# Lower halves of the hidden activations moved from GpSimd to VectorE, and eight accumulator banks dealt out anew

## The chip, the cores and the metric

The kernel runs on one core of a Trainium2 chip. The metric is device time in microseconds (us) of one execution; lower is better. The engines are named as the profile names them: PE is TensorE (matmul), PEld its weight load, DVE is VectorE, ACT is ScalarE, POOL is GpSimd, SP is SyncE, which issues most of the DMAs. Matmul results stand in eight banks of PSUM; POOL does not read them in this kernel.

## The reference

Three layers in a row, on batches of 576 tokens with 512 features, 8 batches in all:

```
q_s = softmax(q, over features); k_s = softmax(k, over tokens)
x   = q_s @ (k_s^T @ v)                      # linear attention, 8 heads of 64
x   = x + relu(layer_norm(x) * g @ w_ch1) @ w_ch2      # 512 -> 2048 -> 512
out = sum over the top 2 of 4 experts of gate * causal_attention(x; wq, wk, wv) @ wo
```

All of it is float32. The kernel splits each float32 operand of a matmul into a high and a low half (type fp32r), and adds three products (high x high, high x low, low x high). The low half is the operand minus its high half, so every operand that a matmul reads costs one pass for the high half and one for the low half.

## The kernel before, in words

The work has three stages. Up to about 250 us the first two batches go through the attention layer and the feed-forward layer, and the weights are prepared. From about 250 to 808 us the batches 2 to 7 go through the feed-forward layer ("fast" batches), one batch in about 90 us, while beside it the attention layer and the layer norm of the next batch are made. From 808 us on the expert layer runs. The change touches the second stage alone.

A fast batch has three groups. In a group (`fast_group`) four blocks of 128 hidden columns are made by seven products of half-size matrices instead of eight; the products run j = 0 to 6, each for i = 0 and 1, and each of these is 6 matmuls into one bank. The products accumulate into three banks by turns: `pa` takes j = 0, 2, 4 and 6, `pc` takes j = 1 and 3, `pb` takes j = 5. Between products, ACT copies a running sum out (`copy`, L1330, tiles `tmp`), and DVE adds such a copy to a later running sum (`total`, L1343). Four of the finished hidden blocks belong to the second half of the tokens (h = 1, tile `hid`), four to the first half (h = 0, they lie in tile `xw_a`). `out_` (L1333) makes relu and the two halves of each. For h = 0 that is `relu_split` (L311): ACT writes relu as the high half (L312), DVE subtracts it and writes the low half (L313). For h = 1 it was three instructions: ACT makes relu in place (L1338), ACT copies it as the high half (L1339), POOL subtracts and writes the low half (L1340).

After the group comes `second` (L1395): eight sums, four for h = 1 and then four for h = 0, each of 12 matmuls into one bank, which DVE then adds to `xT` (L1406). The first of them reads `hid`. In order of need these are `hid` block 0, 2, 1, 3.

The eight banks: four of pool `ps_acc` (acc0 to acc3), two of `ps_m`, two of `ps_y`. Before the change, `pa` had acc0 and acc1 (by i), `pc` and `pb` acc2 and acc3; the eight sums went through one bank of `ps_m` and acc2, acc3, acc0, acc1, in the order that `SBANK` gives. The other bank of `ps_m` was kept for the layer norm's variance `pvar` (`lnbank`). The attention work beside the groups took its banks through `psy` (L340) from the two banks of `ps_y`.

That attention work is done in units, one for two heads of a batch (`Heads`, L419): the pieces name their matmuls `pkm` (L463, L481), `pq` (L548), `pkv` (L554 and L191) and `po` (L191), and the steps of VectorE between them are L453, L499, L505 (row maximum, row sum, reciprocal of q), L449, L472, L490 (k), L540, L571, L572, L581 (halves of the results). POOL makes L456 and L510 of a unit, ACT L475, L494, L537, L577, L598.

SP loads k and q of a later unit (L399, L401) when the buffer of an earlier unit is read, v (L412, L414) when the `pkv` of the unit before it is done, and the prepared weights of the products (`w_r`, L1308) into a ring of five tiles, each when the product that used the tile before is done. SP issues in the order of the program text.

The instructions of PE, DVE, ACT and POOL are put in order by a scheduler that goes through the whole program, by data, buffers and its own estimates of durations; each engine then runs its list in order and waits at an instruction whose inputs or buffers aren't there. A wait so holds up all that stands behind it on that engine.

Of the kernel before, what the change touches and what calls it, by code (L numbers as in the profile page):

```python
# [7 lines left out]
F32 = mybir.dt.float32  # L8
# [3 lines left out]
AF = mybir.ActivationFunctionType  # L12
ALU = mybir.AluOpType
# [5 lines left out]
P = 128  # L19
# [31 lines left out]
FAST = 2  # L51
# [88 lines left out]
def tile_kernel(ctx: ExitStack, tc: tile.TileContext, q, k, v, g_ln, w1, w2, w_gate, wq, wk, wv, wo, out):  # L140
    nc = tc.nc
# [11 lines left out]
    T = S // NH  # L153
# [12 lines left out]
    def raw(ap):  # L166
        return ap.bitcast(F32)
# [42 lines left out]
    ps_m = ctx.enter_context(pool("ps_m", 2, space=PSUM))  # L210
# [100 lines left out]
    def relu_split(ps, h, lo):  # L311
        nc.scalar.activation(h, ps, AF.Relu)  # L312
        nc.vector.scalar_tensor_tensor(lo, ps, 0.0, raw(h), op0=ALU.max, op1=ALU.subtract)  # L313
# [21 lines left out]
    lp = p1r.enter_context(pool("ln", side="right"))  # L335
    ap = p1r.enter_context(pool("a", 2, side="right"))

    spare, idle, lnbank = [], [], []

    def psy(name):  # L340
        if spare:

            spare.append(spare.pop(0))
            if spare[-1] is not None:
                return ps_acc.tile([P, 512], F32, tag=spare[-1], name=name)
        return ps_y.tile([P, 512], F32, tag="y", name=name)


# [284 lines left out]
    class Norm:  # L633
# [25 lines left out]
            nc.vector.tensor_tensor(self.s[:, 1], self.t, raw(self.s[:, 0]), op=ALU.subtract)  # L659

        def mean(self, nm):
            ps = (lnbank[0] if lnbank and nm == "pvar" else psy(nm))[:, :T]
            setattr(self, nm, ps)
            mean_of(ps, self.s)

# [530 lines left out]
    NG = FSPLIT // 4  # L1196
# [76 lines left out]
    def last_space():  # L1273
        x_pair(XORD[5:])
        p1b.close()
        mixp = p1.enter_context(pool("mix"))
        later.append(mixp)
        xslot["b12"] = mixp.tile(XSL, F32R, tag="b12", name="xw_b")
        t = mixp.tile([P, 4, 2, T], F32R, tag="hid", name="hid")
        hid1.extend(t[:, i] for i in range(4))  # L1280
        ring[MIDB] = mixp.tile(WSL, F32R, tag="w", name="w_r")
        qt_odd.append(mixp)
        stream.use(0, before_last + 7, ring)
        stream.fill(-1)
        for _ in range(3):
            t = raw(hp.tile([P, 2, T], F32R, tag="hh", name="tmp", bufs=3))
            temps.extend([t[:, 0], t[:, 1]])
        lnbank.append(ps_m.tile([P, 512], F32, tag="m", name="pvar"))

    class Stream:  # L1290

# [19 lines left out]

    stream = Stream()
    def bank(name, n):
        if n < 0:
            if not main:
                main.append(ps_m.tile([P, 512], F32, tag="m", name="acc"))
            return main[0][:, :T]
        return ps_acc.tile([P, 512], F32, tag=f"acc{n}", name=name)[:, :T]

    main = []  # L1320
    SBANK = (-1, 2, 3, 0, 1, -1, 2, 3)

    def fast_group(b, gr):

        base = (b - FAST) * 7 * NG + 7 * gr
        box = [{} for _ in range(2)]

        def copy(ps, i, k):
            t = temps[3 * i + k]
            nc.scalar.activation(t, ps, AF.Copy)  # L1330
            return t

        def out_(src, i, n, h):  # L1333
            u = (hid0, hid1)[h][2 * i + n]
            if h == 0:
                relu_split(src, u[:, 0], u[:, 1])
                return
            nc.scalar.activation(src, src, AF.Relu)  # L1338
            nc.scalar.activation(u[:, 0], src, AF.Copy)  # L1339
            nc.gpsimd.tensor_tensor(u[:, 1], src, raw(u[:, 0]), op=ALU.subtract)  # L1340

        def total(ps, t):
            nc.vector.tensor_tensor(t, ps, t, op=ALU.add)  # L1343
            return t

        def product(j, i):
            d = box[i]
            nm = ("a", "c", "a", "c", "a", "b", "a")[j]
            begins = nm not in d
            if begins:  # L1350
                d[nm] = bank("p" + nm, i if nm == "a" else 2 + i)
            x, w = xslot[XORD[j]], stream.got[base + j][:, i]
            for c in range(2):
                onto(d[nm], w[:, 0, c], x[:, 0, c], begins and c == 0, False)
                onto(d[nm], w[:, 0, c], x[:, 1, c], False, False)
                onto(d[nm], w[:, 1, c], x[:, 0, c], False, c == 1)
            if j == 0:
                d["t1"] = copy(d["a"], i, 0)
            elif j == 1:
                d["v5"] = copy(d["c"], i, 1)  # L1360
            elif j == 2:
                d["u2"] = copy(d["a"], i, 2)
            elif j == 3:
                out_(total(d["c"], d["u2"]), i, 0, 1)
            elif j == 4:
                out_(total(d["a"], d["v5"]), i, 1, 1)
            elif j == 5:
                out_(total(d["b"], d["t1"]), i, 0, 0)
            else:
                out_(d["a"], i, 1, 0)  # L1370
            if i == 1:
                stream.fill(base + j)

        return [(6, lambda j=j, i=i: product(j, i)) for j in range(7) for i in range(2)]

    def plain_group(b):

        parts = (("b11", "b21"), ("b12", "b22"))

        def one(f, h):  # L1380
            while wide.at < 2 * (f - FSPLIT) + 2:
                wide.step()
            ps = bank("psh", (0, 1, 2, 3, -1)[(4 * (1 - h) + f) % 5])
            for c in range(NDC):
                wh, wl = (w1s[f][:, i, c, :] for i in (0, 1))
                x = xslot[parts[h][c // 2]]
                mm(ps, wh, x[:, 0, c % 2], c == 0, False)
                mm(ps, wh, x[:, 1, c % 2], False, False)
                mm(ps, wl, x[:, 0, c % 2], False, c == NDC - 1)
            u = (hid0, hid1)[h][f - FSPLIT]  # L1390
            relu_split(ps, u[:, 0], u[:, 1])

        return [(12, lambda f=f, h=h: one(f, h)) for h in (1, 0) for f in range(FSPLIT, NFC)]

    def second(b, f0, final):  # L1395

        def one(h, c):
            ps = bank("acc", SBANK[4 * (1 - h) + c])
            sl = slice(c * P, (c + 1) * P)
            for n, i in enumerate((0, 2, 1, 3)):  # L1400
                wt, u = w2s[f0 + i], (hid0, hid1)[h][i]
                mm(ps, wt[:, 0, sl], u[:, 0], n == 0, False)
                mm(ps, wt[:, 0, sl], u[:, 1], False, False)
                mm(ps, wt[:, 1, sl], u[:, 0], False, n == 3)
            xs = xTs[b][:, :, h * T:(h + 1) * T]
            nc.vector.tensor_tensor(xs[:, c], xs[:, c], ps, op=ALU.add)  # L1406
            if final and b == LAST:
                if h not in x2s_last:
                    x2s_last[h] = x_hl(xhlp, "x2")
                x2 = x2s_last[h]  # L1410
                split(xs[:, c], x2[:, 0, c], x2[:, 1, c])
            elif final and c == NDC - 1:
                nc.scalar.dma_start(out=xp_d[b, h], in_=xs)

        return [(12, lambda h=h, c=c: one(h, c)) for h in (1, 0) for c in range(NDC)]
# [79 lines left out]
    n = 2 * HALF + HALF  # L1495
# [3 lines left out]
    m = mixes[FAST]  # L1499
# [5 lines left out]
    for b in range(FAST, B):  # L1505
        if b < LAST:
            slots, n = fronts.pop(b + 1), END
            if b + 2 < B:
                fronts[b + 2] = front(b + 2)
                begin(b + 2, slots, n)  # L1510
        else:
            slots, n = {}, 4 * NFC
            p1r.close()
            x2s_last[0] = t = x_hl(xtp, "x2")
            t = t.rearrange("p a b c -> p (a b c)")
            stream.use(before_last + 7, before_last + 7 * NG, [cut(t, 8 * P * i, WSL) for i in range(2)] + ring[MIDB:] +
                       [later[2].tile(WSL, F32R, tag="qT", name="w_r")])
            wcp = late.enter_context(pool("w_c", side="right"))
            moe["vg"] = wcp.tile([P, 2, NDC, VG], F32R, name="wvg")
            blocks = []  # L1520
            for f in range(FSPLIT, NFC):
                blocks += fc_tiles(wcp, f)
            wide = Wide(blocks, mid, hp, AHEAD)
            conv = calls(wide.step)
            todo = [conv] * len(blocks)
            for s in range(2):
                for r in range(NR):
                    todo.append(calls(lambda s=s, r=r: load_wqk(s, r)))
            for r in range(NR):
                todo.append(calls(lambda r=r: load_wv(r)))  # L1530
            todo.append(calls(load_g))
            for i, g in enumerate(todo):
                slots.setdefault(8 + 2 * i, []).append(g)
        pieces = fast_pieces(b)
        run_pieces(pieces, slots, n)
    p1.close()


# [511 lines left out]
    for n, b in enumerate(order):  # L2050
        side, tail, at_last = back(b, res)
        if n + 1 < B:
            nb = order[n + 1]
            x2s, res = {}, {"plain": n + 2 == B, "beside": n + 2 < B}
            main = mlp2(nb, 0, x2s) + mlp2(nb, 1, x2s) + qk_proj(0, x2s, res)
# [38 lines left out]
```

## Time and profile before

| | us |
|---|---|
| median of 3 runs | 1357.99 (1356.85 to 1361.51) |
| profiled execution | 1363.46, of it 1361.7 in the span |
| PE busy | 1305.5 (96% of the span) |
| DVE busy | 960.0 (70%) |
| ACT busy | 763.2 (56%) |
| POOL busy | 460.6 (34%) |

The span is the time from the first to the last instruction of the profiled execution. A group of instructions is named by its source line, engine, operation and tiles (`out<-in`), with tile numbers left out. An entry in brackets at the end of a timeline row is the time for which the engine sat idle just before it, and what ended the wait. The granted clock of PE (PEclk) is the share of the full clock in a stretch of time; of its two levels, 2.4 GHz counts as 1.00 and 1.2 GHz as 0.50.

### The profile page before, as it was taken

How to read it: one execution, taken by the hardware profiler on the slowest of the kernel's cores; microseconds unless marked ns; L12 is line 12 of the kernel's file. 1: busy time of each engine (PE TensorE's matmuls, PEld its weight loads, DVE VectorE, ACT ScalarE, POOL GpSimd, SP SyncE). 2: the span in 40 equal slices, each digit the busy share in tenths (PEclk: the TensorE clock that was granted, in tenths of full speed). 3: DMA queues.
4: the chain of work that ended last, by engine and by line, in shares of the span. 5: the costliest groups of instructions: out<-in, count | busy, mean ns of one | idle time of the engine just before them, and what ended most of it. 6: DMA issues, size and time to landing. Idle time of an engine off the chain costs nothing.

```text
span 1361.7 us, 27542 instructions
## 1 busy us (share of the span) xinstructions
PE 1305.5 (96%) x9907; PEld 1254.6 (92%) x9907; DVE 960.0 (70%) x2704; ACT 763.2 (56%) x1956; POOL 460.6 (34%) x568
## 2 busy tenths in 40 slices
PE   7899999799999989999999999999999999999998
PEld 6789989689989989999999999999999999999996
DVE  5896666866858759668476537777777777777774
ACT  4875434555555446555456425666666566566665
POOL 5577245443434334434245201112121212121222
PEclk9999999799999989989999999999999999999999
DMA  8763377645855748558348415233324242333122
GB/s 207 235 213 102 109 253 242 214 129 203 266 180 185 222 137 273 161 200 282 113 152 292 118 44 145 78 114 82 89 89 103 92 107 96 82 113 82 48 52 73
DMA packets 173416, 203.53 MB, mean 149 GB/s; under 512 B 93152, under 2 KB 137696, under 8 KB 170976
## 3 DMA queue, kind: packets, MB, share of 16 engines
q1 hardware_dynamic: 150656, 164.80, 40.7%
q10 hardware_dynamic: 22624, 36.97, 7.5%
q8 instruction: 79, 1.29, 0.4%
q14 instruction: 57, 0.47, 0.1%
HBM read 140.13 MB, written 46.40 MB: 137 GB/s over the span
## 4 chain that ended last, share of the span: by engine, by line
PE 79%; DVE 6%; DMA 3%; ACT 2%; issue 1%; SPq 1%; POOL 0%; DVEq 0%; ACTq 0%; POOLq 0%
PE acc L191 20%; PE psh L191 11%; PE psqk L191 7%; PE psc L191 7%; PE pa L194 7%; PE pssc L191 4%; PE py L191 4%; PE pso L191 4%; PE psv L191 4%; PE pc L194 3%; PE pst L1843 3%; PE pb L194 2%; DMA q<-in_q_dram 2%; PE po L191 2%; PE pkv L191 1%
## 5 line engine op out<-in xcount | busy, mean ns | idle before, releaser
L191 PE MATMUL psh<-xhl,w 128*128 128x288 f32 x1248 | 189.0, 298 | 1.3 <-DVE xhl L708 1.0
L191 PEld LDWEIGHTS psh<-xhl,w 128*128 128x128 f32 x1248 | 172.6, 188 | 4.0 <-DVE xhl L708 1.5
L1826 POOL TENSOR_SCALAR sm<-sm,st,lg 128x128 f32<-128x128 f32 (+3 forms) x128 | 82.0, 650 | 264.3 <-DVE st L1823 64.4
L191 PE MATMUL acc<-hid,w 128*128 128x288 f32 x912 | 139.5, 303 | 13.6 <-POOL hid L1340 9.0
L191 PEld LDWEIGHTS acc<-hid,w 128*128 128x128 f32 x912 | 128.5, 192 | 16.0 <-POOL hid L1340 10.1
L191 PE MATMUL acc<-xw_a,w 128*128 128x288 f32 x918 | 129.9, 296 | 0.0
L191 PEld LDWEIGHTS acc<-xw_a,w 128*128 128x128 f32 x918 | 124.1, 188 | 0.3
L191 PE MATMUL psqk<-x,wqk 128*128 128x288 f32 x768 | 112.9, 298 | 0.4 <-DVE k L1646 0.4
L1406 DVE TENSOR_TENSOR xT<-xT,acc 128x288 f32<-128x288 f32 x152 | 66.7, 448 | 60.6 <-PE acc L191 59.5
L191 PEld LDWEIGHTS psqk<-x,wqk 128*128 128x128 f32 x768 | 105.1, 188 | 1.6 <-PE pst L1843 0.6
L191 PE MATMUL psc<-hb,w 128*128 128x288 f32 x672 | 100.2, 298 | 0.0
L1814 ACT ACTIVATE sm<-sm,st 128x128 f32<-128x128 f32 (+3 forms) x144 | 83.9, 584 | 20.6 <-DVE st L1806 19.0
L191 PEld LDWEIGHTS psc<-hb,w 128*128 128x128 f32 x672 | 92.1, 188 | 0.3
L191 PE MATMUL acc<-hh,w 128*128 128x288 f32 x576 | 88.5, 302 | 3.8 <-ACT hh L802 2.2
L1340 POOL TENSOR_TENSOR hid<-tmp,hid 128x288 fp32r<-128x288 f32 x72 | 62.9, 881 | 85.0 <-ACT hid L1339 61.4
L191 PEld LDWEIGHTS acc<-hh,w 128*128 128x128 f32 x576 | 80.2, 190 | 6.4 <-ACT hh L802 2.9
L1867 ACT ACTIVATE aTh<-pst 128x128 fp32r<-128x128 f32 (+4 forms) x224 | 70.2, 333 | 23.5 <-PE pst L1843 11.0
L1868 DVE TENSOR_TENSOR aTl<-pst,aTh 128x384 fp32r<-128x384 f32 (+3 forms) x196 | 72.4, 381 | 11.4 <-ACT aTh L1867 9.0
L1806 DVE CUSTOM_DVE_ANT_0 sm<-pssc,mask 128x128 f32<-128x128 f32 (+2 forms) x144 | 67.9, 482 | 16.0 <-PE pssc L191 6.5
L652 POOL TENSOR_TENSOR sq<-sq 128x288 f32<-128x288 f32 x42 | 38.3, 913 | 103.2 <-ACT sq L683 90.2
L194 PE MATMUL pa<-xw_a,w_r 128*128 128x288 f32 x408 | 65.0, 301 | 1.6 <-ACT xw_a L200 1.0
L194 PE MATMUL pa<-xm,w_r 128*128 128x288 f32 x408 | 63.8, 298 | 1.1 <-DVE pw L272 1.1
(266 smaller groups left out, 3159.0 us busy)
## 6 DMA issues: line engine op xcount, KB each, us to landing
w_r<-w_d SPq DMA_DIRECT2D x118, 512.0 KB, 4.8
wraw<-in_moe_w_ch_dram SPq DMA_DIRECT2D x32, 512.0 KB, 4.7
xhl<-xn_d SPq DMA_DIRECT2D x14, 1152.0 KB, 5.1
xp_d<-xT ACTq DMA_DIRECT2D x16, 576.0 KB, 4.1
k<-k SPq DMA_DIRECT2D x32, 288.0 KB, 3.6
k<-in_k_dram SPq DMA_DIRECT2D x32, 256.0 KB, 3.5
q<-in_q_dram SPq DMA_DIRECT2D x32, 256.0 KB, 4.1
out_dram<-ot SPq DMA_DIRECT2D x32, 256.0 KB, 2.0
```

What stands on the lines that cost most here:

```text
L191: nc.tensor.matmul(o, lhsT, rhs, start=start, stop=stop)
L194: nc.tensor.matmul(o, lhsT, rhs, start=start, stop=stop, skip_group_check=True)
L652: nc.gpsimd.tensor_tensor(self.t, self.t, self.sq[:, c], op=ALU.add)
L1340: nc.gpsimd.tensor_tensor(u[:, 1], src, raw(u[:, 0]), op=ALU.subtract)
L1406: nc.vector.tensor_tensor(xs[:, c], xs[:, c], ps, op=ALU.add)
L1806: nc.vector.tensor_tensor_reduce(out=sm[:m, c0:c1], in0=o_, in1=msk, scale=1.0, scalar=3e38 if n == 0 else st[:m, j, 0:1], op0=ALU.add, op ...
L1814: nc.scalar.activation(sm[:m, :w], sm[:m, :w], AF.Exp, bias=st[:m, j, last:last + 1], scale=-1.0, accum_out=st[:m, j, 2:3])
L1826: nc.gpsimd.tensor_scalar(sm[:m, :w], sm[:m, :w], st[:m, j, 3:4], self.gate()[:, j:j + 1], op0=ALU.mult, op1=ALU.mult)
L1843: nc.tensor.transpose(pt[:kw, kb * m:kb * m + m], sm[:m, kb * P:kb * P + kw], ident[:m, :m])
L1867: nc.scalar.activation(oh, from_, AF.Copy)
L1868: nc.vector.tensor_tensor(ol, from_, raw(oh), op=ALU.subtract)
```

## The change

In words: all lower halves of the hidden blocks are made by DVE (`relu_split` for h = 1 too), so L1338 to L1340 go, and L312 and L313 take their place. The products and the eight sums share the four banks of `ps_acc`, and which bank has which role changes from group to group (`chain_bank`, `sum_bank`); the bank of `ps_m` that one sum used is no longer taken. `pvar` has no bank of its own. `psy` deals out banks of `ps_y` and of `ps_m` by turns, so the units go round four banks instead of two. The plain group of the last batch goes round four banks instead of five.

```diff
-    spare, idle, lnbank = [], [], []
+    spare, idle, more_banks = [], [], []
 
     def psy(name):
...
+        if more_banks:
+            more_banks.append(more_banks.pop(0))
+            if more_banks[0]:
+                return ps_m.tile([P, 512], F32, tag="m", name=name)
         return ps_y.tile([P, 512], F32, tag="y", name=name)
...
         def mean(self, nm):
-            ps = (lnbank[0] if lnbank and nm == "pvar" else psy(nm))[:, :T]
+            ps = psy(nm)[:, :T]
...
-        lnbank.append(ps_m.tile([P, 512], F32, tag="m", name="pvar"))
+        more_banks.extend([0, 1])
...
     def bank(name, n):
-        if n < 0:
-            if not main:
-                main.append(ps_m.tile([P, 512], F32, tag="m", name="acc"))
-            return main[0][:, :T]
         return ps_acc.tile([P, 512], F32, tag=f"acc{n}", name=name)[:, :T]
 
-    main = []
-    SBANK = (-1, 2, 3, 0, 1, -1, 2, 3)
+    def chain_bank(b, gr, nm, i):
+        return (2 * ((b - FAST) * NG + gr) + (0 if nm == "a" else 2) + i) % 4
+
+    def sum_bank(b, gr, n):
+        return (2 * ((b - FAST) * NG + gr) + 2 + n) % 4
...
         def out_(src, i, n, h):
             u = (hid0, hid1)[h][2 * i + n]
-            if h == 0:
-                relu_split(src, u[:, 0], u[:, 1])
-                return
-            nc.scalar.activation(src, src, AF.Relu)
-            nc.scalar.activation(u[:, 0], src, AF.Copy)
-            nc.gpsimd.tensor_tensor(u[:, 1], src, raw(u[:, 0]), op=ALU.subtract)
+            relu_split(src, u[:, 0], u[:, 1])
...
-                d[nm] = bank("p" + nm, i if nm == "a" else 2 + i)
+                d[nm] = bank("p" + nm, chain_bank(b, gr, nm, i))
...
-            ps = bank("psh", (0, 1, 2, 3, -1)[(4 * (1 - h) + f) % 5])
+            ps = bank("psh", (4 * (1 - h) + f) % 4)
...
-            ps = bank("acc", SBANK[4 * (1 - h) + c])
+            ps = bank("acc", sum_bank(b, f0 // 4, 4 * (1 - h) + c))
...
+    more_banks.clear()
     p1.close()
```

The scheduler's order changes all through the second stage on PE, DVE, ACT and POOL; SP's order is the same, and so is every engine's order from the expert layer on. In the rows of the changed kernel the line numbers are its own (L1341 is `total`, L544 is L540 of before, L503 is L499, L457 is L453, L509 is L505). The place shown is the second group of the second fast batch.

PE before, from the last unit piece ahead of the sums to the last products (`acc<-hid` are sums of h = 1):

```order
L554 MATMUL pkv_4703<-ident,qe_4638 128x128
L191 MATMUL pkv_4703<-v_140,ke_4630 64x66 x10
L191 MATMUL acc<-hid,w_4_157 128x288 x3
L191 MATMUL acc<-hid,w_6_593 128x288 x2
L191 MATMUL po_4749<-qT_4686,kv_1961 128x288 x2
L191 MATMUL acc<-hid,w_6_593 128x288
L191 MATMUL acc<-hid,w_5_158 128x288 x3
L191 MATMUL acc<-hid,w_7_594 128x288
L191 MATMUL po_4749<-qT_4686,kv_1961 128x288
L191 MATMUL po_4754<-qT_4686,kv_1961 128x288 x3
L191 MATMUL acc<-hid,w_7_594 128x288 x2
L194 MATMUL pb<-xm,w_r 128x288 x12
```

PE in the changed kernel, from the same unit's `pkv` (here number 4695) to the first sum of h = 1:

```order
L191 MATMUL pkv_4695<-v_140,ke_4621 64x66 x10
L194 MATMUL pc<-xm,w_r 128x288 x6
L194 MATMUL pa<-xw_a,w_r 128x288 x12
L194 MATMUL pc<-xw_a,w_r 128x288 x12
L194 MATMUL pa<-xw_a,w_r 128x288 x12
L191 MATMUL po_4741<-qT_4678,kv_1961 128x288 x2
L191 MATMUL po_4746<-qT_4678,kv_1961 128x288 x2
L191 MATMUL po_4741<-qT_4678,kv_1961 128x288
L191 MATMUL po_4746<-qT_4678,kv_1961 128x288
L194 MATMUL pb<-xm,w_r 128x288 x12
L194 MATMUL pa<-xm,w_r 128x288 x12
L191 MATMUL acc<-hid,w_4_157 128x288 x3
```

The products j = 5 and 6 (`pb` and the last `pa`, 24 matmuls) now stand ahead of the first sum, and the unit's `pkv` stands 42 matmuls of products ahead of `pb` where it stood right ahead of the first sum.

DVE before, in the same group, from the first `total` on:

```order
L1343 TENSOR_TENSOR tmp<-pc,tmp 128x288
L1343 TENSOR_TENSOR tmp<-pa,tmp 128x288
L453 TENSOR_REDUCE sm_5357<-q_4641 128x10
L1343 TENSOR_TENSOR tmp<-pc,tmp 128x288
L1343 TENSOR_TENSOR tmp<-pa,tmp 128x288
L540 TENSOR_TENSOR qT_4686<-pq_4681,qT_4686 128x4x112
L540 TENSOR_TENSOR qT_4686<-pkv_4703,qT_4686 128x128
L571 TENSOR_SCALAR ks_4720<-pkv_4703 128x2
L572 RECIPROCAL ks_4720<-ks_4720 128x2
L499 TENSOR_REDUCE sm_5357<-q_4641 128x10
L581 SCALAR_TENSOR_TENSOR kv_1961<-pkv_4703,ks_4720,kv_1961 64x64
L505 RECIPROCAL sm_5357<-sm_5357 128x10
```

DVE in the changed kernel, from the first `total` of that group on:

```order
L1341 TENSOR_TENSOR tmp<-pc,tmp 128x288
L503 TENSOR_REDUCE sm_5347<-q_4632 128x10
L1341 TENSOR_TENSOR tmp<-pc,tmp 128x288
L313 SCALAR_TENSOR_TENSOR hid<-tmp,hid 128x288
L1341 TENSOR_TENSOR tmp<-pa,tmp 128x288
L509 RECIPROCAL sm_5347<-sm_5347 128x10
L1341 TENSOR_TENSOR tmp<-pa,tmp 128x288
L313 SCALAR_TENSOR_TENSOR hid<-tmp,hid 128x288 x2
L1341 TENSOR_TENSOR tmp<-pb,tmp 128x288
L313 SCALAR_TENSOR_TENSOR hid<-tmp,hid 128x288
L1341 TENSOR_TENSOR tmp<-pb,tmp 128x288
L313 SCALAR_TENSOR_TENSOR xw_a<-tmp,xw_a 128x288
```

L457, the step that waits for a load of q, now stands ahead of the group's first `total` (it is not in the piece shown), L503 stands behind that `total`, and the four lower halves `hid<-tmp,hid` stand between the totals.

## Rows read from the trace of the kernel before

**Rows 1.** Page, busy us, share of the span, instructions.

```profile
PE 1305.5 (96%) x9907; PEld 1254.6 (92%) x9907; DVE 960.0 (70%) x2704; ACT 763.2 (56%) x1956; POOL 460.6 (34%) x568
```

**Rows 2.** Waits of PE from 262 to 807 us: total us, times, longest.

```profile
PE acc L191 <- POOL hid L1340: 9.0, 5, 3.5
PE pc L194 <- issue: 4.9, 4, 1.4
PE pc L194 <- DVE xm L201: 3.6, 2, 2.1
PE acc L191 <- ACT hid L1339: 3.2, 2, 2.0
PE acc L191 <- DVE xw_a L313: 1.3, 1, 1.3
```

**Rows 3.** Timeline of all engines, 390 to 402 us: PE's sums, and POOL.

```profile
394.09 0.66 PE L191 MATMUL acc<-hid,w 128*128 128x288 f32 x3
...
395.70 1.41 POOL L510 TENSOR_TENSOR qe<-q,sm 128x320 f32<-128x320 f32 x2
...
395.97 0.40 PE L191 MATMUL acc<-hid,w 128*128 128x288 f32 x1 [1.22 <-ACT hid L1339]
...
397.06 1.56 POOL L1340 TENSOR_TENSOR hid<-tmp,hid 128x288 fp32r<-128x288 f32 x2
...
397.91 0.40 PE L191 MATMUL acc<-hid,w 128*128 128x288 f32 x1 [1.54 <-POOL hid L1340]
```

**Rows 4.** Chain of waits, 385 to 403 us: start, us, what.

```profile
386.51 0.74 DVE k L490
...
389.73 2.98 DMA q<-in_q_dram
...
392.83 0.06 DVE sm L453
...
397.07 0.83 DVE sm L499
```

**Rows 5.** Windows: us, PE, PEld, DVE, ACT, POOL busy (instructions), PEclk, DMA share, GB/s.

```profile
303.00:314.00 11.00, 7.46 (x35) 7.23 (x36) 5.13 (x14) 4.78 (x13) 6.45 (x8) 0.69 0.77 265
314.00:326.00 12.00, 12.00 (x92) 12.00 (x92) 6.39 (x15) 3.96 (x9) 2.43 (x3) 1.00 0.29 89
394.30:405.30 11.00, 7.93 (x44) 7.27 (x44) 5.72 (x16) 6.02 (x17) 5.89 (x8) 0.84 0.81 276
485.20:496.20 11.00, 7.60 (x36) 7.06 (x37) 5.40 (x15) 5.85 (x16) 5.97 (x8) 0.69 0.76 267
576.20:588.20 12.00, 9.22 (x43) 8.54 (x44) 5.60 (x15) 6.34 (x18) 6.08 (x9) 0.72 0.75 254
326.00:357.00 31.00, 29.75 (x234) 28.89 (x233) 29.66 (x51) 17.43 (x38) 15.40 (x14) 1.00 0.74 247
```

**Rows 6.** Groups from 262 to 808 us: busy us, mean ns, idle before.

```profile
L1343 DVE TENSOR_TENSOR tmp<-pa,tmp 128x288 f32<-128x288 f32 x36 | 16.0, 454 | 10.1 <-PE pa L194 10.0
L1340 POOL TENSOR_TENSOR hid<-tmp,hid 128x288 fp32r<-128x288 f32 x72 | 62.9, 881 | 85.0 <-ACT hid L1339 61.4 <-PE pc L194 16.4 <-PE pa L194 6.8
L1339 ACT ACTIVATE hid<-tmp 128x288 fp32r<-128x288 f32 x72 | 30.9, 437 | 0.8
```

**Rows 7.** Line L313, 262 to 808 us: ns min/median/max.

```profile
L313 DVE SCALAR_TENSOR_TENSOR xw_a<-tmp,xw_a x36: 396/563/1470, 276.3 to 775.3; 128x288 fp32r<-128x288 f32 x36
L313 DVE SCALAR_TENSOR_TENSOR xw_a<-pa,xw_a x36: 435/445/458, 279.0 to 776.7; 128x288 fp32r<-128x288 f32 x36
```

**Rows 8.** Timeline of PE, 322 to 362 us: the batch's first `pc`.

```profile
356.68 1.03 PE L194 MATMUL pc<-xm,w_r 128*128 128x288 f32 x6 [1.25 <-issue]
```

**Rows 9.** Timeline of SP, 355 to 450 us.

```profile
394.07 1.25 SPq L412 DMA_DIRECT2D v<-in_v_dram  x2
...
396.02 33.72 SPq L1308 DMA_DIRECT2D w_r<-w_d  x14
```

**Rows 10.** Page, DMA issues: KB each, median us from issue to landing.

```profile
w_r<-w_d SPq DMA_DIRECT2D x118, 512.0 KB, 4.8
```

**Rows 11.** Timeline of PE, 240 to 330 us: last wait at the start of the stage.

```profile
262.86 2.77 PE L194 MATMUL pc<-xm,w_r 128*128 128x288 f32 x10 [2.14 <-DVE xm L201]
```

## Prediction

> **What bounds the kernel now.** I read the page's busy times first, then the waits of PE over the fast batches, then the timeline and the chain of waits at the longest of them, and last the windows, for what the clock does there. PE is busy for 96% of the span, and no other engine for more than 70% [rows 1]. So what can be won is PE's idle time and the time in which it runs at the lower clock, and both are small. The reader is to see in the waits [rows 2] that the largest sum has one cause: the first sums of a group wait for the `hid` halves, 9.0 us for POOL's low half and 3.2 us for ACT's high half, 12.2 us in all.
>
> These waits lie at four places, the second group of four of the six fast batches. At the second place [rows 3] PE stands at the first sums from 394.75 us (394.09 and 0.66) with two waits, 1.22 and 1.54, and POOL makes the low halves only after it has made a unit's L510. Further back [rows 4], the chain goes through a load of q that lands at 392.7 and for which L453 waits at the head of DVE's list. The totals stand behind L453, and the last two low halves behind POOL's unit work.
>
> After each of these places the granted clock falls: 0.69, 0.84, 0.69 and 0.72 over the stretches that hold the waits [rows 5]. It stays at 1.00 in the stretch of a batch's end, though PE waits there too, for 1.25 us in one piece [rows 5, 8]. At full clock 92 matmuls take 12.00 us, 0.130 each [rows 5]. The four stretches hold 35, 44, 36 and 43 matmuls, which would take 4.6, 5.7, 4.7 and 5.6 us. PE was busy with them for 7.46, 7.93, 7.60 and 9.22. The lower clock so cost 2.9, 2.2, 2.9 and 3.6, together 11.6 us.
>
> **The change part by part.** *Low halves on DVE.* 72 POOL instructions (62.9 us) and 72 of ACT (30.9 us) go [rows 6]; 72 of DVE come, L313 with both inputs in SBUF. The trace has 36 such, from 0.396 to 1.470 us with a median of 0.563, where the 36 with one input in PSUM lie between 0.435 and 0.458 [rows 7]. I take 0.6 each, 43 us over 546 us, between the bounds 0.4 and 1.47. DVE is no bound on average.
>
> The Trainium skill (page "SBUF — State Buffer", section "Who interferes with whom") says that a VectorE instruction with two SBUF inputs and a GpSimd instruction that reads SBUF shut each other out for a whole instruction. The trace agrees: only the form with two SBUF inputs is spread out [rows 7]. That speaks against this change, since all 72 are of that form; it speaks for it in that the 72 POOL instructions that go were themselves of the kind that shuts DVE out. By the rule alone, with those 72 gone, the new instructions would come near the shortest row, some 29 us in all instead of 43; neither figure moves the sum, since DVE has room for both on average.
>
> *Does the first sum still wait?* The price of a late low half is counted from the order. The last product that feeds `hid` (`pa`, j = 4) is now followed by `pb` and `pa`, 24 matmuls, and the last block is read after 9 matmuls of the first sum: 33 x 0.130 = 4.3 us. In that time DVE has to do the total (0.45, rows 6), ACT the relu (0.44, taken from L1339 in rows 6), DVE two earlier low halves (1.2), one total of `pb` (0.45) and the last low half (0.6), which makes 3.1 us. The margin is 1.2 us. Before, nothing stood between that product and the first sum but a unit's `pq` and `pkv`. So the 12.2 us go, and with them the 11.6 of the clock, if no wait of over about 1.5 us stays there; waits of up to 1.4 left the clock at 1.00 [rows 2, 5].
>
> *What is late next.* In DVE's list L503 (the old L499) stands between the first and the second total of a group, and L499 ended its wait only at 397.07, 4.2 us after L453 [rows 4]. So a unit's q can still hold back the low halves, now in DVE's own list. Two things soften it: the unit stands some 50 matmuls (6.5 us) earlier against the products, and the load of q, issued when an earlier k has been read, comes earlier with it. For what is left, the nearest row is the wait of the sums for DVE's low halves of h = 0, which was 1.3 us, once in 18 groups [rows 2]. The distance there is longer, so I take twice that and a little, 3 us in all. The bounds are 0 and 2.3 us in each of the 15 groups with a unit beside them, 35 us.
>
> *Four banks for units.* This lets `pkv` go ahead of the products. SP issues v and then a product's weights behind it, at 394.07 and 396.02, 1.95 us later [rows 9], and a weight tile lands 4.8 us after its issue [rows 10]. From `pkv` to `pb` there are now 42 matmuls and 6 of `po`, 48 x 0.130 = 6.2 us, against 1.95 + 4.8 = 6.8. So the weights of `pb` come 0.5 us late or just in time, which is within the 3 us. Before, they were hidden behind the wait for `hid`. That cover is gone: were they 2.5 us late, it would cost 2 us more at each of six places.
>
> *Sums and products on four banks.* A sum's bank is needed again four sums later (48 matmuls, 6.2 us), and the next group's `pc` needs the banks of the last two sums, as before. So the waits at a batch's end (4.9 us in four places, labelled issue, for a bank that DVE frees [rows 2, 8]) stay. There DVE is busy for 29.66 of 31 us [rows 5]. Four low halves add 2.4 us there. Against it stand four POOL instructions of 0.88 that no longer stretch DVE's others, and unit work that the order puts elsewhere. I take nothing, between -5 (all gone) and +10 (2 us more at each of five places).
>
> *The start of the stage.* The waits up to 262.86 [rows 11] hang on the split of the first fast batch's inputs, and are left as they are (bounds -4 and +4). `pvar` without its own bank and `psh` on four banks cost nothing: a `psh` is 12 matmuls, and its bank is needed 6.2 us later.
>
> **The sum.** 12.2 + 11.6 - 3 = 20.8 us less. The profiled execution took 1363.46 us, 1361.7 of it in the span, so its like would take 1342.7. It lay 5.5 above the median of 1357.99; the same 20.8 from the median gives 1337.
>
> **The rivals.**
>
> *A: the wait changes hands.* DVE's list is held at L457 or L503 by q's load, and the sums wait for DVE about half as long as for POOL. For it: L453's wait stood at the root of the chain [rows 4]. Against it: the unit stands earlier, and the margin is 1.2 us. Half of 23.8 is won, less 3: 1349.
>
> *B: the weights of `pb` are what ends last.* For it: 6.8 us against 6.2. Against it: only the tiles of finished products are issued, one or two instead of the 14 in a row of rows 9. Six places at 2 us on top of the forecast: 1349.
>
> *C: DVE's low halves come too late everywhere, and the kernel is slower.* Place: the first sum of each of 15 groups. The low half takes as long as the longest of its kind, 1.47 us [rows 7], when POOL's unit work runs beside it. Four are then 4 x 0.87 = 3.5 us later than reckoned, 2.3 beyond the margin, 35 us in 15 groups: 1358 - 23.8 + 35 = 1369. It outweighs the gain from a mean of about 1.3 us on: 23.8 / 15 = 1.6, and 1.6 + 1.2 = 2.8, a quarter of it 0.7 above 0.6. Against it: the median is 0.563, with the POOL halves still there.
>
> *D: nothing is won.* The order was made with estimates, and another place takes the whole gain, such as five batch ends that each wait 2 us longer and so lose clock too, 5 x (2 + 2.5, a little under the mean of the four clock costs) = 22: 1359.
>
> **How the numbers follow.** Forecast 0.58, A 0.15, B 0.10, C 0.12, D 0.05. The forecast's own range is 1328 to 1346. Below it lie cases in which the batch ends or the start also gain. The range that should hold 8 in 10 is 1322 to 1358: it leaves out C, most of D and a few in a hundred below. A measurement of this kernel tells about 0.3% (4 us) from no change. Faster: the forecast and nine in ten of A and B, 0.81. Same: the rest of A and B and most of D, 0.07. Slower: C, 0.12.
>
> **What would show it.** Right: no wait of `acc<-hid` for POOL; those for DVE's `hid` under 4 us in all; PEclk at 1.00 in the second groups of all fast batches; `hid<-tmp,hid` on L313 at a mean of 0.45 to 0.7 us; `pc` at the batch ends waiting about 1.2 us each. A would show as waits of `acc` for DVE `hid` with L503 late behind POOL's L460, B as waits of `pb` for DMA `w_r`, C as a mean of `hid` on L313 over 1.3 us and waits in nearly all groups, D as waits of `pc` or `pa` at the batch ends of over 3 us. The forecast is wrong if the clock still falls in the second groups, or if PE's idle time from 262 us to the end of the fast batches is not at least 8 us less.

## The result, and the profile after

| | before | changed |
|---|---|---|
| median, us | 1357.42 (1355.09 to 1361.51, 4 runs) | 1344.12 (1342.0 to 1345.61, 4 runs) |
| ratio, 95% interval | | 0.9898 (0.987 to 0.9925) |
| span of the profiled execution | 1361.7 | 1341.8 |

The kernel is faster by 13.3 us. A second comparison (`after_again` below) gave 0.9884 (0.9861 to 0.9906). Both ratios together put the gain at about 15 us; I had forecast 20.8.

The page's busy times after answer to [rows 1]:

```profile
PE 1295.0 (97%) x9907; PEld 1244.7 (93%) x9907; DVE 979.2 (73%) x2776; ACT 738.4 (55%) x1884; POOL 403.0 (30%) x496
```

The 72 instructions went from POOL and ACT to DVE as announced. PE is busy for 10.5 us less with the same 9907 matmuls; about half of that lies in the second stage (below), the other half ahead of it. The waits of PE after, from 262 to 807 us (total us, times, longest), answer to [rows 2]:

```profile
PE pc L194 <- ACT tmp L1333: 3.8, 2, 2.4
PE acc L191 <- DVE tmp L1341: 3.6, 4, 1.6
PE acc L191 <- DVE xT L1404: 3.2, 4, 0.9
PE pa L194 <- DVE wvg L201: 0.5, 1, 0.5
PE pa L194 <- ACT tmp L1333: 0.3, 1, 0.3
```

No wait for a `hid` half is left, neither POOL's nor DVE's, and the four waits of `pc` labelled issue are gone too. In their place the sums wait for DVE in two new ways: for the total of `pb` (L1341), whose bank the second sum takes, and for the addition to `xT` (L1404), which frees the bank of an earlier sum.

The place that answers to [rows 3] is shown here in the first fast batch, where [rows 2] had the longest wait (3.5 us). Timeline after, 301 to 316 us (start, us, engine, line, what):

```profile
300.78 0.46 DVE L313 SCALAR_TENSOR_TENSOR hid<-tmp,hid 128x288 fp32r<-128x288 f32 x1 [0.39 <-ACT hid L312]
...
302.12 0.96 DVE L313 SCALAR_TENSOR_TENSOR hid<-tmp,hid 128x288 fp32r<-128x288 f32 x1
...
303.74 0.44 DVE L313 SCALAR_TENSOR_TENSOR hid<-tmp,hid 128x288 fp32r<-128x288 f32 x1
...
304.47 0.44 DVE L313 SCALAR_TENSOR_TENSOR hid<-tmp,hid 128x288 fp32r<-128x288 f32 x1
...
304.97 6.51 PE L191 MATMUL acc<-hid,w 128*128 128x288 f32 x48
```

The first sums start at 304.97 with no wait, and all 48 matmuls of h = 1 run in one piece. The lower half of the last block ends at 304.91, and the first sum reads that block only after 9 matmuls (1.2 us): the margin that I had reckoned, 1.2 us, is what the trace shows here.

The granted clock, which had fallen at four second groups [rows 5], stays at 1.00 over all four of them (columns as in [rows 5]):

```profile
300.00:330.00 30.00, 30.00 (x228) 29.66 (x226) 24.48 (x52) 16.64 (x40) 8.44 (x10) 1.00 0.50 171
385.00:415.00 30.00, 30.00 (x229) 30.00 (x229) 22.62 (x51) 15.71 (x37) 8.30 (x9) 1.00 0.54 186
472.00:502.00 30.00, 30.00 (x229) 29.77 (x228) 24.48 (x51) 16.39 (x39) 8.44 (x10) 1.00 0.51 177
558.00:588.00 30.00, 30.00 (x230) 30.00 (x229) 22.65 (x50) 15.68 (x38) 8.29 (x9) 1.00 0.54 179
```

Line L313 after, 262 to 807 us (ns min/median/max), answers to [rows 7]:

```profile
L313 DVE SCALAR_TENSOR_TENSOR hid<-tmp,hid x72: 434/450/1208, 267.2 to 753.3; 128x288 fp32r<-128x288 f32 x72
L313 DVE SCALAR_TENSOR_TENSOR xw_a<-tmp,xw_a x36: 436/449/1370, 274.8 to 754.8; 128x288 fp32r<-128x288 f32 x36
L313 DVE SCALAR_TENSOR_TENSOR xw_a<-pa,xw_a x36: 431/448/466, 275.1 to 755.2; 128x288 fp32r<-128x288 f32 x36
```

To see where the time went, the fast stage is cut out whole, from the first `pc` to the first `psv` of the expert layer (columns as above: length, busy us of PE, PEld, DVE, ACT, POOL with instructions, PEclk, DMA share, GB/s). Before:

```profile
257.80:826.10 568.30, 541.96 (x4190) 528.86 (x4191) 382.68 (x763) 287.99 (x670) 217.98 (x234) 0.97 0.58 185
```

After:

```profile
253.60:805.40 551.80, 536.73 (x4188) 522.56 (x4189) 402.51 (x833) 262.92 (x597) 160.71 (x162) 0.99 0.60 192
```

The stage is 16.5 us shorter: PE's idle time went from 26.3 to 15.1 us (11.3 less), and its busy time from 542.0 to 536.7 (5.2 less). The two spans differ by 19.9 us. Of the other 3.4, 4.2 lie ahead of the stage, where two executions of before alone differ by 2.7 (`before_look` below), and 0.8 go the other way behind it.

### The profile page after: what moved, and what is told of

Its sections match the earlier page's. It is cut to its first block, busy times and chain, and to the rows that moved or that the text cites. A ratio compares the mean times of both kernels' runs of the same rounds, so it can differ in the third digit from the quotient of the medians.

```text
span 1341.8 us, 27486 instructions
## 1 busy us (share of the span) xinstructions
PE 1295.0 (97%) x9907; PEld 1244.7 (93%) x9907; DVE 979.2 (73%) x2776; ACT 738.4 (55%) x1884; POOL 403.0 (30%) x496
## 4 chain that ended last, share of the span: by engine, by line
PE 77%; DVE 9%; DMA 5%; ACT 2%; issue 1%; SPq 1%; POOL 0%; DVEq 0%; ACTq 0%; POOLq 0%
PE acc L191 18%; PE psh L191 11%; PE psqk L191 7%; PE psc L191 7%; PE pa L194 6%; PE pssc L191 4%; PE py L191 4%; PE pso L191 4%; PE psv L191 4%; PE pc L194 3%; PE pst L1842 3%; DMA q<-in_q_dram 2%; PE po L191 1%; PE pb L194 1%; DVE km L453 1%
## 5 line engine op out<-in xcount | busy, mean ns | idle before, releaser
L191 PE MATMUL acc<-hid,w 128*128 128x288 f32 x912 | 128.0, 297 | 3.6 <-DVE tmp L1341 3.6
L191 PEld LDWEIGHTS acc<-hid,w 128*128 128x128 f32 x912 | 123.0, 188 | 5.0 <-DVE tmp L1341 4.5
L1404 DVE TENSOR_TENSOR xT<-xT,acc 128x288 f32<-128x288 f32 x152 | 66.9, 445 | 40.0 <-PE acc L191 39.4
L514 POOL TENSOR_TENSOR qe<-q,sm 128x320 f32<-128x320 f32 x64 | 46.9, 752 | 86.4 <-PE pkv L558 43.4
```

The costliest lines, as they stand in the source:

```text
L191: nc.tensor.matmul(o, lhsT, rhs, start=start, stop=stop)
L514: nc.gpsimd.tensor_tensor(self.qe[:, :, j, :], self.qt[:, j], self.sm[:, 2, j * NCH:(j + 1) * NCH, None].to_broadcast([P, NCH, D]), op=ALU ...
```

## The experiments

Theories at the start. **1**: POOL's list made the lower halves late, so moving them to DVE is the gain. **2**: the gain is in the order, because the new banks let the last products and the unit's work stand ahead of the first sums. **3**: half and half. The stage column is the stretch from the first `pc` to the first `psv` of the one profiled execution, with PE's idle time in it.

| run | lower halves of h = 1 | banks | median, us | ratio to before, 95% | stage; PE idle; PE busy |
|---|---|---|---|---|---|
| before, first and second profile | POOL | old | 1357.42 | | 568.3; 26.3; 542.0 and 570.2; 26.5; 543.7 |
| changed, first profile | DVE | new | 1344.12 | 0.9898 (0.987 to 0.9925) | 551.8; 15.1; 536.7 |
| after_again | DVE | new | 1344.44 | 0.9884 (0.9861 to 0.9906) | 553.0; 16.3; 536.8 |
| e1_dve_only | DVE | old | 1363.94 | 1.0044 (1.0025 to 1.0063) | 572.3; 26.9; 545.4 |
| e2_banks_only | POOL | new | 1339.92 | 0.9862 (0.9844 to 0.9879) | 548.3; 10.9; 537.4 |
| e2_again | POOL | new | 1341.87 | 0.986 (0.9838 to 0.9882) | 549.0; 11.8; 537.3 |
| e3_two_unit_banks | DVE | shared four, units on two | 1383.44 | 1.0178 (1.016 to 1.0197) | 591.1; 46.5; 544.6 |
| e4_three_unit_banks | DVE | old sums, units on three | 1349.27 | 0.9931 (0.9915 to 0.9948) | 559.7; 20.6; 539.2 |
| e8_three_banks_pool | POOL | old sums, units on three | 1350.87 | 0.9935 (0.9919 to 0.9952) | 558.3; 19.9; 538.5 |
| e5_pool_h0 | DVE (36 of h = 0 on POOL) | new | 1343.77 | 0.9865 (0.9839 to 0.9891) | 555.8; 17.6; 538.2 |
| e6_pool_all | POOL (36 of h = 0 too) | new | 1340.96 | 0.9856 (0.9835 to 0.9878) | 547.0; 9.4; 537.6 |
| e9_double | DVE, written twice | new | 1360.57 | 1.001 (0.9997 to 1.0023) | 568.6; 24.7; 543.9 |

Each ratio stands against runs of before on the same chip; the medians of before there were 1359.09 (e1 to e4), 1361.62 (the set with after_again) and 1360.01 (e8, e9).

**e1: the halves alone.** Against before:

```diff
-            if h == 0:
-                relu_split(src, u[:, 0], u[:, 1])
-                return
-            nc.scalar.activation(src, src, AF.Relu)
-            nc.scalar.activation(u[:, 0], src, AF.Copy)
-            nc.gpsimd.tensor_tensor(u[:, 1], src, raw(u[:, 0]), op=ALU.subtract)
+            relu_split(src, u[:, 0], u[:, 1])
```

> Before with only the lower halves moved to VectorE; the banks of sums, products and units are those of before. Theory 1 (POOL's list alone was the cause): the waits of the first sums for the lower half go, the clock stays at 1.00 in the second groups, and most of the change's 13.3 us is there: 1344 to 1349. Theory 2 (the new order by the banks did it, because it puts 24 matmuls between the last product that feeds hid and the first sum): the wait changes hands from POOL to DVE, still over 1.5 us at three or four of the four places, and the time is 1352 to 1360. Theory 3 (each part takes away half): 1350 to 1352.

Measured: slower by 0.44%. PE's longest waits, 265 to 815 us, and the windows with the second groups (columns as above):

```profile
PE acc L191 <- DVE hid L313: 10.1, 12, 2.0
PE pc L194 <- ACT tmp L1330: 3.3, 3, 2.6
```

```profile
300.00:330.00 30.00, 28.35 (x188) 27.09 (x189) 20.16 (x46) 12.73 (x31) 9.46 (x11) 0.89 0.53 173
390.00:420.00 30.00, 27.48 (x178) 25.96 (x179) 19.79 (x43) 12.88 (x30) 7.92 (x10) 0.89 0.50 159
480.00:510.00 30.00, 26.64 (x188) 24.45 (x187) 19.00 (x43) 11.61 (x27) 7.23 (x9) 0.89 0.46 146
570.00:600.00 30.00, 26.59 (x193) 25.73 (x192) 18.02 (x40) 12.24 (x28) 8.40 (x10) 0.89 0.47 155
```

The wait changed hands: 9.0 us for POOL's half in five waits became 10.1 for DVE's in twelve, and the clock falls in all four second groups as before. Theory 1 fell, and theory 2's expectation of the mechanism came true (1.9, 2.7, 2.9 and 2.0 us of these waits at the four places); the time came out above every range.

**e2: the banks alone.** The changed kernel with the six removed lines above put back.

> The changed kernel with POOL making the lower halves of h = 1 again, as before; the banks are the new ones. Theory 1 (POOL's list alone): the first sums still wait for POOL's hid, the clock still falls in second groups, 1354 to 1362. Theory 2 (the order by the banks): POOL now has 33 matmuls (4.3 us) for it, the wait for hid goes at most places, 1344 to 1349. Theory 3 (each half): 1349 to 1353.

Measured: 0.9862, and 0.986 the second time. PE's waits, 240 to 815 us, hold none for POOL's `hid`; the longest behind the start of the stage are

```profile
PE pa L194 <- DVE xT L1409: 1.5, 4, 0.6
PE pa L194 <- ACT tmp L1333: 1.2, 1, 1.2
```

The stretch in which the first sums of [rows 5] waited now runs at full clock without a gap (columns as above):

```profile
303.00:314.00 11.00, 11.00 (x86) 11.00 (x85) 7.53 (x14) 4.39 (x11) 5.79 (x7) 1.00 0.41 142
```

POOL needs 0.87 us for a lower half as before, and it is in time: `pb` and the last `pa` stand ahead of the sums here too. PE's timeline of e2:

```profile
301.40 1.76 PE L194 MATMUL pb<-xm,w_r 128*128 128x288 f32 x12
303.00 1.76 PE L194 MATMUL pa<-xm,w_r 128*128 128x288 f32 x12
304.60 1.09 PE L191 MATMUL acc<-hid,w 128*128 128x288 f32 x7
```

So theory 2 holds: the banks carry the whole gain and the moved halves none of it. Banks and order weren't changed apart, since the scheduler makes the order from the banks; that the order is what does it is read from these rows. The effects about add up: e1's +0.44% and e2's -1.38% make -0.94%, beside -1.02% and -1.16% for the changed kernel.

**e3: four unit banks taken back.** The changed kernel with

```diff
-            ps = psy(nm)[:, :T]
+            ps = (lnbank[0] if lnbank and nm == "pvar" else psy(nm))[:, :T]
...
-        more_banks.extend([0, 1])
+        lnbank.append(ps_m.tile([P, 512], F32, tag="m", name="pvar"))
```

> The changed kernel with the units on two banks and pvar in a bank of its own, as before; lower halves on DVE and the four shared banks stay. If the four unit banks are needed (the unit's pq and pkv move away from the sums only by them, and the load of q with them): DVE's hid halves stand behind the unit's steps again, the sums wait for DVE hid by 1 to 3 us at some of the four places, 1348 to 1354. If the four shared banks and the moved halves do it all: 1342 to 1346, the same as the changed kernel.

Measured: 24.4 us above before by the medians, worse than either expectation, and by another wait than I had named. PE's longest wait, 265 to 836 us, and a timeline of the first of the four places:

```profile
PE po L191 <- ACT kv L581: 22.6, 4, 6.1
```

```profile
301.87 0.80 PE L191 MATMUL pkv<-v,ke 112*64 112x66 f32 x20
...
303.22 0.82 DVE L457 TENSOR_REDUCE sm<-q 128x10 f32<-128x640 f32 x1 [2.46 <-DMA q<-in_q_dram]
303.95 0.95 DVE L544 TENSOR_TENSOR qT<-pq,qT 128x448 fp32r<-128x448 f32 x1
...
304.81 0.45 DVE L1341 TENSOR_TENSOR tmp<-pa,tmp 128x288 f32<-128x288 f32 x1
...
307.82 0.29 ACT L581 ACTIVATE kv<-pkv,ks 64x64 fp32r<-64x64 f32 x1
...
308.82 1.09 PE L191 MATMUL po<-qT,kv 128*128 128x288 f32 x3 [6.15 <-ACT kv L581]
```

With two banks `po` stands right behind `pkv` in PE's list, and ahead of `pb`. DVE waits 2.46 us at L457 for the load of q, as at the root of [rows 4], then makes `qT`, totals and lower halves, and `kv` is ready only 6 us after `pkv`. All that the changed kernel puts there, 24 matmuls of `pb` and `pa`, is stuck behind. Before has two unit banks too and is 24 us faster: there `po` stands among the sums. So together with the shared banks the units need their four, which keep the unit's chain out of the way of the products. (e3 leaves one of the eight banks idle, and no run has the shared banks with POOL's halves and two unit banks.)

**e4 and e8: half of the banks.** Before with units on three banks and `pvar` among them, the sums' own bank kept. e4 has the lower halves on DVE, e8 on POOL.

```diff
+        if third:
+            third.append(third.pop(0))
+            if third[0] is not None:
+                return third[0]
...
-        lnbank.append(ps_m.tile([P, 512], F32, tag="m", name="pvar"))
+        third.extend([None, None, ps_m.tile([P, 512], F32, tag="m", name="py3")])
```

> Before with lower halves on DVE, the sums' own main bank kept, pvar among the units, and units going round three banks. It takes away the one wait that the change brought: the second sum of a batch's first group waits for the bank of pb (0.28, 0.64, 1.10 and 1.59 us, 3.6 in all). If that wait costs its length and nothing else is lost: 1339 to 1342, below the changed kernel. If the shared banks are needed for the order (theory 2): DVE's hid halves are waited for again, 1348 to 1356.

> As e4 (sums keep their own main bank, pvar among the units, units on three banks), but POOL makes the lower halves of h = 1 as before: before with one more bank for the units and nothing else. If it is only the units' banks that free the order, and POOL has time enough then: 1340 to 1346. If the shared banks of sums and products are needed to let the last products stand ahead of the sums: POOL's halves are waited for again, 1350 to 1358.

Measured: 0.9931 and 0.9935, alike within their intervals, whoever makes the halves: about half of e2's gain. The sums still wait for `hid`, in e4 for DVE's halves (240 to 815 us):

```profile
PE acc L191 <- DVE hid L313: 3.7, 10, 0.6
```

and in e8 for POOL's (265 to 815 us):

```profile
PE acc L191 <- POOL hid L1344: 4.3, 5, 1.4
```

With POOL's halves a third unit bank (and no bank for `pvar` alone) wins one half, and the fourth, together with the shared banks, the other. With DVE's halves the third wins more, from e1's 1.0044 to 0.9931, about 1.1 of 1.5 to 1.6%. That e4 would beat the changed kernel by sparing it the wait for `pb`'s bank was wrong: that wait went, and larger ones came.

**after_again, e2_again, e5, e6: where the halves should be made.** The changed kernel and e2 once more on one chip, and two kernels that put other lower halves on POOL, by the condition in `out_`:

```diff
-            relu_split(src, u[:, 0], u[:, 1])
+            if h == 1 or n == 1:    # e5; in e6: h == 0 and n == 1
+                relu_split(src, u[:, 0], u[:, 1])
+                return
+            nc.scalar.activation(src, src, AF.Relu)
+            nc.scalar.activation(u[:, 0], src, AF.Copy)
+            nc.gpsimd.tensor_tensor(u[:, 1], src, raw(u[:, 0]), op=ALU.subtract)
```

> The changed kernel, unchanged, beside the three others of this set. 1342 to 1346. If the profiled execution of before was a long one, the gain by medians stays at 12 to 15 us, and the start of the stage (first pc) lies at 252 to 256 us as in the other kernels; if the first profile of after was a slow one, the ratio falls below 0.988.

> The new banks with POOL making the lower halves of h = 1, again, on the same chip as the changed kernel. If the move of the lower halves to VectorE costs something (theory: DVE's list gets 72 instructions longer, and the sums and the next products wait for it): 3 to 6 us below the changed kernel. If the difference was between chips: within 2 us of it.

> The changed kernel with 36 of the 144 lower halves given to POOL: those of h = 0 that come from SBUF (j = 5). Those of h = 1 stay on VectorE. Theory L (the length of DVE's list is what costs): about a quarter to a half of e2's advantage, 1341 to 1343. Theory U (only the halves of h = 1 are urgent, and DVE makes them late): the same as the changed kernel, 1343 to 1346.

> The changed kernel with 108 of the 144 lower halves on POOL: those of h = 1 and those of h = 0 that come from SBUF. Theory L (the length of DVE's list costs): a little below e2, 1336 to 1340. Theory U: the same as e2, 1339 to 1341. Rival (POOL's list is late once it holds 108 instructions of 0.88 us): the sums wait for POOL's hid or xw_a, 1343 to 1352.

Measured: 1344.44, 1341.87, 1343.77 and 1340.96. The changed kernel's gain is 17.2 us by the medians of this set, above the expected 12 to 15; e2's 2.6 us below the changed kernel lie between its two expectations, and e5 and e6 are as theory U has them. The four intervals overlap, so by time alone little is told apart. The profiles say more: PE's idle time in the stage is 15.1 and 16.3 us where DVE makes the halves of h = 1, and 10.9, 11.8 and 9.4 where POOL does. The profile of e5, with 36 instructions less on DVE than the changed kernel, has 17.6. So the bare length of DVE's list (theory L) does not explain it; the idle time goes with who makes the halves of h = 1. That it comes by what stands behind them in DVE's list is likely, since the sums' waits for `pb`'s total are 3.6 us in the changed kernel and 0.3 in e2, but no run shows it alone. Why e5 itself isn't better (its first wait is `pc` for ACT's copies, 7.5 us in six waits) stays open. e2 was below the changed kernel in both comparisons, by 4.2 and 2.6 us of medians from different sets and the same set; e2 and e6 have the lowest medians of this study.

**before_look: was the profile of before a long one?** Nothing changed.

> The kernel before, unchanged, profiled once more. If its first profile was typical of the stage: the stage of the fast batches, from the first pc to the first psv, takes 566 to 569 us again, the granted clock falls at the same four second groups, and only the part before the stage is shorter (first pc at 252 to 256 us in place of 257.83). If the clock's loss was a matter of that one execution: it falls at fewer places, and the stage takes 560 to 565 us.

Measured: 570.2 us for the stage, a little above the expected 566 to 569, the granted clock at 0.89 over 30 us around each of the four second groups, the first `pc` at 255.17. The clock so fell at the same four places, and the stage was 1.9 us longer, not shorter; what the first profile had more, 2.7 us, lies ahead of the stage. So the forecast's clock term was not spoilt by an odd execution.

**e9: the suspected cost doubled.** In the changed kernel, behind `relu_split`:

```diff
+            if h == 1:
+                nc.vector.scalar_tensor_tensor(u[:, 1], src, 0.0, raw(u[:, 0]), op0=ALU.max, op1=ALU.subtract)
```

> The changed kernel with every lower half of h = 1 written twice by VectorE: 72 instructions more, about 0.45 to 0.53 us each, 32 to 38 us on DVE's list. Theory L (DVE's list is what the sums and products now wait for, and 72 instructions cost 3 to 4 us): at least 4 us more, 1348 to 1356. Theory U (the lower halves are hidden, the difference to e2 has another cause): within 2 us of the changed kernel, 1342 to 1347. My rival C (too late in nearly every group): 1365 or more.

Measured: 1360.57, level with before (ratio 0.9997 to 1.0023). PE's longest wait, 265 to 815 us:

```profile
PE acc L191 <- DVE hid L1340: 8.9, 6, 2.0
```

72 instructions of 0.57 us (41 us in all) cost 16 us, above the range of theory L. The gain of the banks is used up once a lower half takes DVE about twice as long.

## Why the prediction was right or wrong

**The time** came out 7 us above the forecast and inside its range. The direction was right; the part that brings the gain was not, and one term of the sum was left out.

**The cause was put to the wrong part.** I wrote that the 12.2 us of `hid` waits go because DVE makes the halves with a margin of 1.2 us. They go (none is left), but the margin comes from the 24 matmuls that the new order puts ahead of the first sum, and POOL meets it too (e2), while DVE without the order does not (e1). The question that I left out was what POOL would do in the new order. Rival A described e1 well. It did not happen in the changed kernel, although the totals there still stand behind waits for q (L457 waited 19.4 us in all after, L453 11.3 before): the products now cover them.

**What the new order adds to PE's own time was put at nothing.** This is the step of the sum that failed. The sum took the 11.6 us of the clock for the whole fall of PE's busy time. That time fell by only 5.2 us in the stage (6.1 as a mean over the two profiles of each). The places themselves were read about rightly. Around the third one, before (columns as above):

```profile
485.00:490.00 5.00, 1.40 (x3) 0.86 (x4) 3.29 (x10) 3.80 (x10) 4.61 (x6) 0.72 0.74 211
490.00:495.00 5.00, 5.00 (x25) 5.00 (x25) 1.48 (x3) 1.35 (x4) 1.56 (x2) 0.59 0.92 369
```

where 5 us at full clock take 40 matmuls. At the four places 81 matmuls began while the granted clock stood at 0.50. Counted from start to start in the trace, without the idle time, they took 20.7 us, and at 0.133 each they would have taken 10.8: 10.0 us were lost, and 12.0 in the second profile of before. The changed kernel lost 1.4 us, at one place of its own in the last batch, behind the wait of 2.4 us of `pc` for ACT's copy:

```profile
720.00:750.00 30.00, 28.45 (x203) 28.46 (x204) 18.38 (x38) 15.17 (x33) 5.93 (x5) 0.94 0.70 202
```

In `after_again` that wait was 0.45 us, and the clock stayed at 1.00. So the clock gave back 8.6 us in the first profiles and 12.0 in the second, near the forecast's 11.6. What came on against it, 3.4 and 5.1 us, is time of the same matmuls at full clock. Over the batch that holds the third place, before:

```profile
446.90:538.40 91.50, 86.84 (x681) 84.21 (x681) 65.38 (x131) 47.57 (x112) 37.91 (x40) 0.96 0.62 200
```

and the like batch after:

```profile
449.40:537.30 87.90, 85.18 (x680) 82.26 (x680) 68.93 (x142) 43.12 (x100) 27.09 (x28) 1.00 0.69 218
```

PE's busy time fell by 1.7 us where I had 2.9 for this place. Much of what came on stands beside the short matmuls of the units (`pkm`, `pq`, `pkv`), which now break up the products at more places. Six matmuls of `pc` in one run, before (387.18 us), and six right behind a unit's `pkv`, after (382.59 us), both at full clock:

```profile
387.18 0.96 PE L194 MATMUL pc<-xm,w_r 128*128 128x288 f32 x6
382.59 1.06 PE L194 MATMUL pc<-xm,w_r 128*128 128x288 f32 x6
```

Over the whole stage, at full clock and from start to start, a 128x288 matmul right behind a short one took 0.22 us in the median, and one among its like 0.133. There were 73 of the first kind before and 87 after; what they took beyond 0.133 went from 6.8 to 8.2 us, and that of the matmuls right ahead of a short one from 1.2 to 2.6. Together that is 2.8 of the 3.4 us of the first profiles, and as much of the 5.1 of the second; the rest is not told apart, and no run changed this alone.

The forecast made the clock hang on a single wait of over about 1.5 us. The runs don't bear that out: at e1's second place no single wait was over 0.77 us (four of them, 2.6 us in all, from 389.1 us on), and the clock fell at 393.6; in the changed kernel a wait of 1.59 us at 622.7 left it at 1.00.

**New waits, and the batch ends.** I had 3 us for new waits and nothing for the batch ends. The idle time in the stage fell by 11.3 us (10.8 as a mean over two profiles each), against a forecast of 9.2. The sum came out near, but not its parts, and that is luck: errors of opposite sign. The 4.9 us of `pc` went, which I had left standing, and waits of the sums for banks came (3.6 and 3.2), which I had put at nothing. I had checked a sum's bank against the next sums, and not the second sum against `pb`, whose total in the first groups of a batch stands behind other work in DVE's list. The longest of these, timeline after, 622 to 627 us:

```profile
621.94 1.26 DVE L453 TENSOR_REDUCE km<-k 128x128 f32<-128x640 f32 x1
...
623.11 0.45 DVE L313 SCALAR_TENSOR_TENSOR xw_a<-tmp,xw_a 128x288 fp32r<-128x288 f32 x1
...
623.75 0.45 DVE L1341 TENSOR_TENSOR tmp<-pb,tmp 128x288 f32<-128x288 f32 x1
...
624.25 2.92 PE L191 MATMUL acc<-hid,w 128*128 128x288 f32 x20 [1.59 <-DVE tmp L1341]
```

Where POOL makes the halves, this wait is 0.3 and 0.5 us in all (the two profiles of e2).

**Rivals B, C and D** did not come. No `pb` or `pa` waits for `w_r` in the first profile after (one of 0.7 us in the second). C's price per late half was about right: it had the gain used up at a mean of about 1.3 us, and in e9, with 1.08 us for both instructions of a block, it was.

**Durations.** The lower half took 0.511 us in the mean (36.4 us busy for the 72), where I had taken 0.6 and 43 us, inside the band of 0.45 to 0.7.

## What to carry to other kernels

When two parts of a change answer the same wait, price each one alone: ask of the old engine, too, whether it would be in time in the new order. An engine that is late at one point of an order is cured by what stands between its input and its reader, and more banks for the side work may buy just that. A clock loss read at one place is the gain there; for the whole, ask too what a new order costs the busiest engine at full clock, since the same matmuls may take longer where others break up their runs.

## What the runs showed of the hardware

Where POOL has more to do, DVE's form with both inputs in SBUF takes longer, and only that form. With POOL making the lower halves of h = 1 (e2, 262 to 801 us; busy us, mean ns):

```profile
L1343 POOL TENSOR_TENSOR hid<-tmp,hid 128x288 fp32r<-128x288 f32 x72 | 61.6, 872 | 103.8 <-ACT hid L1342 67.2 <-PE pa L194 26.1 <-DVE tmp L1346 10.5
L313 DVE SCALAR_TENSOR_TENSOR xw_a<-tmp,xw_a 128x288 fp32r<-128x288 f32 x36 | 27.2, 759 | 3.6 <-ACT xw_a L312 3.2
L313 DVE SCALAR_TENSOR_TENSOR xw_a<-pa,xw_a 128x288 fp32r<-128x288 f32 x36 | 15.1, 443 | 0.0
```

In the changed kernel the same form (`xw_a<-tmp,xw_a`) takes 599 ns in the mean (21.6 us over 36) and the form with one input in PSUM 447. Over all kernels the first form's mean is 456 to 654 where DVE makes the halves of h = 1 and POOL only its other work, and 675 to 768 where POOL makes those of h = 1 (e5 and e6, where POOL makes this one itself, left aside). The rule that the prediction drew on (the Trainium skill, page "SBUF — State Buffer", section "Who interferes with whom") agrees in sign with these rows. It did not decide anything: e2, with the longer DVE instructions, has the shorter stage.

The time from the start to the first `pc` was between 250.3 and 257.8 us over the profiles of this study. Before and e1, whose lists for PE are the same up to that point, gave 257.8, 255.2 and 252.3. What makes it differ was not tried.

A 128x288 matmul right behind a short one (112 to 128 rows, 66 to 128 columns) took 0.22 us from start to start at full clock, and 0.133 among its like (medians; stage of before and of the changed kernel, both profiles of each).
